# Four transposing loads in place of eight TensorE transposes, and the weights on one queue

## The chip, the cores and the metric

The kernel runs on one core of a Trainium2 chip. The metric is the device time of one execution in microseconds (us). The kernel before took 262.44 us (median of 3 runs, 262.2 to 262.47).

A core has five engines that run their own lists of instructions in order: TensorE (PE, with its weight loads listed apart as PEld), VectorE (DVE), ScalarE (ACT), GpSimd (POOL) and SyncE (SP). SP issues transfers, and ScalarE issues some beside its own work. The two have a queue each; 16 transfer engines work off both.

## What is computed

The reference mixes two branches of the same input x (2048 tokens of 512 channels, bf16) by a gate per token:

```python
x = A_x
g = _sigmoid((x * gate_w).sum(-1, keepdims=True))
a = _A_ref(x, A_wq, A_wk, A_wv, A_wo, A_beta)
b = _B_ref(x, B_w_gate, B_w_up, B_w_down)
return g * a + (1 - g) * b
```

Branch A is attention with a memory, for 32 heads of 16 channels, over four segments of 512 tokens one after the other:

```python
logits = jnp.einsum('bhqd,bhkd->bhqk', qs, ks) * scale + mask
p = _softmax(logits, axis=-1)
a_dot = jnp.einsum('bhqk,bhkd->bhqd', p, vs)
pq = phi(qs)
num = jnp.einsum('bhld,bhde->bhle', pq, M)
den = jnp.einsum('bhld,bhd->bhl', pq, z)[..., None] + 1e-06
a_mem = num / den
o = g * a_mem + (1.0 - g) * a_dot
...
pk = phi(ks)
M = M + jnp.einsum('bhld,bhle->bhde', pk, vs)
z = z + jnp.einsum('bhld->bhd', pk)
```

Branch B is a gated feed-forward layer: `h = gelu(x @ w_gate) * (x @ w_up)`, and `h @ w_down`, with 1792 hidden channels.

## The kernel before

**Tiling.** The work is split into the four segments s = 0 to 3 of 512 tokens. x is needed with channels on the partitions: `xT` holds it as four blocks kb of 128 channels by 512 tokens. For each segment there are tasks by name: `K{s}_{t}`, `Q{s}_{t}`, `V{s}_{t}` (projections, t = 0 to 3), `G{s}_{ft}` and `U{s}_{ft}` (gate and up projections, 14 each), `qk{s}_{t}...` (fills of scores into four PSUM banks called psXALL, five for each t that is even and four for each odd one), `exp...` (ScalarE, 128x2048 at a time), `msk...` (GpSimd), `pv...` (probabilities times V), `norm...`, `mz`, `numx` and `num` (memory), and `D`, `R` (down and output projections). The other four PSUM banks, psW, are shared by all other results. `...ev` tasks copy a result out of PSUM to SBUF.

**Order.** Every task is created by `_build`, and `ORDER` (L43 to L144) lists by hand, for each engine, in which order its tasks run, and so which of ScalarE and VectorE does each copy. `Sched.schedule` (L269) goes along these lists to give out the PSUM banks; it uses a table of assumed landing times, `LANDING` (L39), for the first transfers. `Emitter` (L349 on) derives the semaphore waits from what each task reads and writes. Every engine works in order, so that an instruction that waits holds all behind it.

**Tiling modes of TensorE.** Fills of scores, `numx` and the row pieces `R` use 32 rows of the array at a time; `pv` and `mz` use 32 columns at a time. `Sched.column_runs` also splits the wide matmuls of a stretch between two fills by columns when the stretch holds a `pv` or `mz` (L543 in the profile instead of L541). `Sched.change` names what counts as a change of mode.

**The head.** While x and the weights come in, TensorE runs eight matmuls on constants (`warm0` to `warm7`, L635). The first segment's x is loaded as plain rows into `xin` (four blocks of hT[1]) by two transfers, `x0_0` for tokens 0 to 255 and `x0_1` for tokens 256 to 511 (L578). Each half is transposed by TensorE with eight 128x128 matmuls into psXALL (`x0t0a_u`, `x0t0b_u`, `x0t1_u`, L644) and copied into `xT` by VectorE and ScalarE (`x0ev...`, L651 and L652). K of this segment is computed in pieces of 256 columns, so that a piece needs one half u of x only: `K0_t.0` and `.1` are blocks 0 and 1 of the first half, `.2` and `.3` of the second, `.4` and `.5` blocks 2 and 3 of the first, `.6` and `.7` of the second. `Q0_t` goes to psXALL, in 512 columns; `Q0_t.0` needs the first half of wq, `Q0_t.2` the second. The first fill of scores, `qk0_0A0`, needs all of psXALL free again.

wk comes in three transfers (`w_wk0`, `w_wk1`, `w_wk2`), wq and wv in two. SP issues x0_0, x0_1, w_wk2, w_wq1, w_wv1, then the first half of w_gate (w_wg0), the x of the next segment as four transposing loads (`x1_0` to `x1_3`, L574), the gate's weights `gwb` and `beta`, and the second half of w_gate. ScalarE issues w_wk0, w_wk1, w_wq0 and w_wv0.

`xin` is read a second time: VectorE multiplies it with gwb (`gmul0`, L806), and the row sums of that give the gate.

Of the kernel before, what the change touches and what calls it, by code (L numbers as in the profile page):

```python
# [21 lines left out]
P = 128  # L22
# [17 lines left out]
    "x0_0": 4.35, "w_wk0": 4.15, "x0_1": 5.6, "w_wk1": 5.45, "w_wk2": 6.6, "w_wq0": 7.0, "w_wq1": 8.4, "w_wv0": 9.2,  # L40
    "w_wv1": 10.2, "w_wg0": 12.2, "x1_0": 12.9, "w_gwb": 13.2, "x1_1": 13.8, "w_beta": 14.1, "x1_2": 14.4, "x1_3": 14.8,
# [1220 lines left out]
```

## Time and profile before

| | |
|---|---|
| median of the runs | 262.44 us (262.2, 262.44, 262.47) |
| profiled execution | 262.03 us |
| its span, first to last instruction | 260.8 us |
| granted TensorE clock, mean | 1.0 |
| TensorE busy, 0 to 10 us | 8.73 us |
| TensorE busy, 10 to 20 us | 9.95 us |
| first transpose of x0 | 4.52 us |
| first matmul of K0, of Q0 | 5.19 us, 8.18 us |
| first fill of scores, first exp | 13.35 us, 13.80 us |

The first transfers, with the time at which each was issued and how much later it had landed:

| transfer | queue | issued | landed after |
|---|---|---|---|
| x0_0, 256 KB | SP | 0.82 | 3.7 |
| w_wk0, 128 KB | ACT | 0.87 | 3.4 |
| w_wk1, 128 KB | ACT | 1.30 | 4.2 |
| x0_1, 256 KB | SP | 1.32 | 4.4 |
| w_wk2, 256 KB | SP | 1.82 | 5.3 |
| w_wq0, 256 KB | ACT | 1.82 | 5.5 |
| w_wq1, 256 KB | SP | 2.33 | 6.3 |
| w_wv0, 256 KB | ACT | 2.34 | 6.6 |
| w_wv1, 256 KB | SP | 2.84 | 6.7 |
| w_wg0, 896 KB | SP | 3.35 | 8.7 |
| x1_0, transposing | SP | 3.87 | 8.7 |

In the views, a row of the timeline begins with its start and length in us; then follow engine, source line, operation, what it writes and reads, how many instructions were merged in it, and in brackets the idle time before it and what ended it. L541 is any wide matmul, L543 one that is split by columns, L920 a fill of scores, L1088 a row piece.

### The profile page before, as it was taken

The numbers are of one execution on the slowest core, as the hardware profiler recorded it, in microseconds if no ns is written. First come the engines' busy times: TensorE is split into PE (matmuls) and PEld (weight loads), VectorE is DVE, ScalarE is ACT, GpSimd is POOL, SyncE is SP. The second block draws the span as 40 slices with busy tenths as digits, with TensorE's granted clock in tenths as the row PEclk, the third lists the DMA queues.
The fourth block names the chain that finished last, engine by engine and source line by source line (L and its number), as shares of the span: only waits on it lengthen the run. The fifth ranks groups of instructions, "written<-read, shape, count | busy, mean of one in ns | idle before, by whom it ended". The sixth has DMA issues, their size and how long they took to land.

```text
span 260.8 us, 10396 instructions
## 1 busy us (share of the span) xinstructions
PE 254.2 (97%) x4653; PEld 126.9 (49%) x4674; DVE 183.8 (70%) x348; ACT 212.4 (81%) x191; POOL 104.8 (40%) x260
## 2 busy tenths in 40 slices
PE   8999999999999999999999999999999999999996
PEld 3544354444553664534454563544455445454454
DVE  0688789989997616989889307899898301598563
ACT  4699899899999969988849867889988878877722
POOL 8206484878000544193800008548310128526430
DMA  7963263069049022190005303020000300320002
GB/s 217 318 173 61 45 186 103 3 213 195 3 49 238 14 53 63 23 124 3 3 3 120 64 5 92 15 85 1 3 4 14 93 5 0 85 64 3 3 3 83
DMA packets 32780, 18.43 MB, mean 71 GB/s; under 512 B 20576, under 2 KB 32736, under 8 KB 32736
## 3 DMA queue, kind: packets, MB, share of 16 engines
q1 hardware_dynamic: 31904, 16.99, 27.8%
q8 instruction: 36, 0.59, 0.9%
q10 hardware_dynamic: 832, 0.79, 0.9%
q14 instruction: 8, 0.07, 0.1%
HBM read 9.84 MB, written 2.10 MB: 46 GB/s over the span
## 4 chain that ended last, share of the span: by engine, by line
PE 89%; DVE 4%; ACT 2%; DMA 1%; issue 1%; POOL 0%; ACTq 0%
PE psW L541 33%; PE psW L543 24%; PE psW L1088 14%; PE psXALL L920 8%; PE psW L968 5%; PE psXALL L543 2%; DMA hT<-in_A_x_dram 1%; PE psXALL L541 1%; ACT pt L926 1%; DVE hT L564 1%; PE psW L976 1%; DVE tb L982 1%; ACT ptl L926 1%; PE psXALL L839 1%; DVE glog L814 0%
## 5 line engine op out<-in xcount | busy, mean ns | idle before, releaser
L926 ACT ACTIVATE pt<-psXALL 128x2048 bf16<-128x2048 f32 x64 | 120.1, 1877 | 25.7 <-PE psXALL L920 23.0
L929 POOL TENSOR_SCALAR_AFFINE_SELECT pt<-pt 128x256 bf16<-128x256 bf16 x128 | 57.5, 461 | 82.9 <-ACT pt L926 77.8
L929 POOL TENSOR_SCALAR_AFFINE_SELECT ptl<-ptl 128x512 bf16<-128x512 bf16 x32 | 23.1, 721 | 52.7 <-ACT ptl L926 51.0
L1067 DVE TENSOR_TENSOR hT<-psW,hT 128x512 bf16<-128x512 f32 x56 | 36.9, 682 | 9.0 <-PE psW L541 7.8
L1088 PE MATMUL psW<-wd,hT 32*128 32x512 bf16 x576 | 34.8, 374 | 0.0
L982 DVE STREAM_TRANSPOSE tb<-psW 128x512 f32<-128x512 f32 x32 | 22.3, 706 | 9.9 <-PE psW L976 9.8
L541 PE MATMUL psW<-xT,wu 128*128 128x512 bf16 x111 | 28.1, 380 | 1.2 <-issue 0.8
L1117 DVE TENSOR_SCALAR ost<-psW,omgt 128x512 bf16<-128x512 f32 x8 | 5.8, 747 | 32.7 <-PE psW L541 31.1
L541 PE MATMUL psW<-xT,wg 128*128 128x512 bf16 x112 | 28.0, 380 | 0.6 <-issue 0.3
L920 PE MATMUL psXALL<-qT,kpad 32*128 32x320 bf16 (+3 forms) x512 | 25.6, 272 | 0.4 <-ACT ptl L926 0.2
L543 PE MATMUL psW<-xT,wu 128*32 128x512 bf16 x424 | 25.9, 379 | 0.0
L543 PE MATMUL psW<-xT,wg 128*32 128x512 bf16 x432 | 25.4, 379 | 0.0
L1088 PEld LDWEIGHTS psW<-wd,hT 32*128 32x128 bf16 x576 | 18.9, 93 | 10.4
L1051 ACT ACTIVATE hT<-psW 128x512 bf16<-128x512 f32 x28 | 15.5, 596 | 6.5 <-PE psW L543 6.0
L920 PEld LDWEIGHTS psXALL<-qT,kpad 32*128 32x128 bf16 x512 | 8.8, 92 | 22.1 <-ACT pt L926 16.0
L968 PE MATMUL psW<-pt,vaug 128*17 128x192 bf16 (+3 forms) x512 | 19.2, 273 | 0.0
L541 PEld LDWEIGHTS psW<-xT,wu 128*128 128x128 bf16 x118 | 10.5, 98 | 13.6 <-issue 1.2
L541 PEld LDWEIGHTS psW<-xT,wg 128*128 128x128 bf16 x116 | 10.5, 98 | 13.0 <-issue 1.9
L968 PEld LDWEIGHTS psW<-pt,vaug 128*17 128x17 bf16 x512 | 11.8, 91 | 9.5 <-issue 0.8
L543 PEld LDWEIGHTS psW<-xT,wu 128*32 128x32 bf16 x424 | 10.9, 97 | 10.3 <-issue 0.4
L926 ACT ACTIVATE ptl<-psXALL 128x2048 bf16<-128x2048 f32 x8 | 15.0, 1880 | 1.0 <-PE psXALL L920 0.8
L543 PEld LDWEIGHTS psW<-xT,wg 128*32 128x32 bf16 x432 | 10.6, 97 | 10.1 <-issue 0.4
(124 smaller groups left out, 385.4 us busy)
## 6 DMA issues: line engine op xcount, KB each, us to landing
out_dram<-ost SPq DMA_DIRECT2D x15, 128.0 KB, 1.8
wg<-in_B_w_gate_dram SPq DMA_DIRECT2D x2, 896.0 KB, 7.2
wu<-in_B_w_up_dram SPq DMA_DIRECT2D x2, 896.0 KB, 6.8
wd<-in_B_w_down_dram SPq DMA_DIRECT2D x2, 896.0 KB, 5.9
phkt<-in_A_x_dram SPq DMA_DIRECT2D x3, 512.0 KB, 4.5
vlow<-vaug SPq DMA_DIRECT2D x8, 136.0 KB, 2.9
hT<-in_A_x_dram SPq DMA_DIRECT2D x2, 256.0 KB, 4.0
wo<-in_A_wo_dram SPq DMA_DIRECT2D x1, 512.0 KB, 6.2
```

The lines of the kernel that those rows point to most:

```text
L541: return e.matmul(view(), lhsT, rhs, start=first, stop=last)
L543: r = e.matmul(view()[c:c + 32, :], lhsT[:, c:c + 32], rhs, start=first, stop=last, tile_position=(0, c))
L564: alts[DVE] = [Instr(lambda e: e.tensor_copy(dst(), src()), reads=reads, writes=writes, est=dve_t(n))]
L920: instrs.append(Instr(lambda e, g=g, lhs=lhs, rhs=rhs, c0=c0, ncol=ncol: e.matmul(X[g][:, c0:c0 + ncol], lhs(32 * g), rhs(32 * g), start=T ...
L926: exp_task(s, f"exp{s}_{t}{name}", [Instr(lambda e: e.activation(dst[:], XALL[:, :].rearrange("p (g c) -> p g c", g=4), ACTF.Exp, scale=AT ...
L929: task(f"msk{s}_{t}{name}", POOL, [Instr(lambda e, view=view, pat=pat, base=base: e.affine_select(out=view, in_=view, compare_op=ALU.is_ge ...
L968: instrs.append(Instr(lambda e, t=t, q=q, kb=kb, slot=slot, c0=c0: e.matmul(gp.f32()[32 * q:32 * q + 17, 128 * kb + 64:512], Vaug[sl][:, k ...
L982: task(f"pvt{s}_{t}_{j}", DVE, [Instr(lambda e: e.transpose(Tb[:, j, :], gp.f32()[:, :]), [gp.key], [("Tb", j)], 0.71)], grp=gp)
L1051: lambda e, g=g, ft=ft, s=s: e.activation(hT[s % 2][:, ft, :], g.f32()[:, :], ACTF.Gelu_apprx_tanh),
L1067: task(f"Um{s}_{ft}", DVE, [Instr(lambda e, g=g, ft=ft: e.tensor_tensor(hT[sl][:, ft, :], g.f32()[:, :], hT[sl][:, ft, :], ALU.mult), [g.k ...
L1088: return Instr(lambda e: e.matmul(gs[tile].f32()[:, :], a[32 * r:32 * r + 32, :], b[32 * r:32 * r + 32, :], start=False, stop=False, tile_ ...
L1117: DVE: [Instr(lambda e: e.tensor_scalar(ost[:], g.f32()[:, :], omgt[:, gt:gt + 1], None, ALU.mult), rd, wr, dve_t(512, ap=True))]}, grp=g))
```

## The change

The second half of x0 goes into `xT[0][:, kb, 256:512]` by four transposing loads `x0T_0` to `x0T_3`, one for each block of 128 channels, which SP issues directly behind x0_0. The three TensorE tasks that transposed it and their copies are gone. `x0_1` remains, since gmul0 reads it, but SP issues it behind w_wg0 and x1_0. All pieces of wk, wq and wv are issued by ScalarE, so that it issues seven transfers instead of four. Every list of `ORDER` is another one, and `LANDING` holds other assumed times.

```diff
-    for u in range(2):
+    rank[0] -= 20000.0
+    dma("x0_0", SP, lambda: xin[:, 0:2, :], lambda: A_x[0, 0:256, :].rearrange("(a p) d -> p a d", p=P), [],
+        [("hT", 1, a) for a in range(2)], 250000, bias=rank[0], issue=0.5)
+    for wkey, i, dst, src in wloads:
+        wdma((wkey, i), ACT, dst, src, 250000, issue=0.5)
+    for kb in range(4):
         rank[0] -= 20000.0
-        dma(f"x0_{u}", SP, lambda u=u: xin[:, 2 * u:2 * u + 2, :],
-            lambda u=u: A_x[0, u * 256:(u + 1) * 256, :].rearrange("(a p) d -> p a d", p=P), [],
-            [("hT", 1, 2 * u + a) for a in range(2)], 250000, bias=rank[0], issue=0.5)
-        for wkey, i, dst, src in wloads[u:u + 1] if u == 0 else wloads[1:]:
-            wdma((wkey, i), SP if (wkey, i) in (("wk", 2), ("wq", 1), ("wv", 1)) else ACT, dst, src, 250000,
-                 issue=0.5)
+        dma(f"x0T_{kb}", SP, lambda kb=kb: xT[0][:, kb, 256:512],
+            lambda kb=kb: A_x[0, 256:512, kb * 128:(kb + 1) * 128], [], [("xT", 0, kb, 1)], 87500,
+            issue=0.7, transpose=True, bias=rank[0])
     wdma(("wg", 0), SP, wg[:, :, 0:half], wgr[:, :, 0:half], 790000)
-    xdma(1, 0, 2)
+    xdma(1, 0, 1)
+    rank[0] -= 20000.0
+    dma("x0_1", SP, lambda: xin[:, 2:4, :], lambda: A_x[0, 256:512, :].rearrange("(a p) d -> p a d", p=P), [],
+        [("hT", 1, 2 + a) for a in range(2)], 250000, bias=rank[0], issue=0.5)
+    xdma(1, 1, 2)
...
-    for nm, u, k0, nk, c0 in (("0a", 0, 0, 1, 0), ("0b", 0, 1, 1, 1024), ("1", 0, 2, 2, 2048),
-                              ("0a", 1, 0, 1, 3072), ("0b", 1, 1, 1, 1280), ("1", 1, 2, 2, 512)):
+    for nm, u, k0, nk, c0 in (("0a", 0, 0, 1, 0), ("0b", 0, 1, 1, 1024), ("1", 0, 2, 2, 2048)):
...
-        held = [("x0ps", c0) for c0 in ((0, 512), (1024, 1280), (2048,), (3072,))[t]] if x else []
+        held = [("x0ps", c0) for c0 in ((0,), (1024,), (2048,), ())[t]] if x else []
```

The lists of TensorE in the head, up to the first fill, and in the stretch of row pieces of the last segment, the old ones first:

```diff
-        "warm0 warm1 warm2 warm3 warm4 warm5 warm6 warm7 x0t0a_0 x0t0b_0 x0t1_0 K0_0.0 K0_2.0 K0_3.0 K0_1.0 "
-        "x0t0a_1 x0t0b_1 K0_3.1 K0_0.1 K0_2.1 x0t1_1 K0_1.1 K0_1.2 K0_3.2 K0_0.2 K0_1.3 K0_1.4 K0_1.5 K0_1.6 "
-        "K0_1.7 K0_0.3 K0_0.4 K0_0.5 K0_0.6 K0_0.7 Q0_3.0 Q0_0.0 K0_3.3 Q0_2.0 Q0_3.2 Q0_2.2 K0_2.2 K0_2.3 Q0_1.0 "
-        "Q0_0.2 Q0_1.2 V0_2.0 V0_2.2 K0_2.4 K0_2.5 K0_2.6 K0_2.7 qk0_0A0 V0_0.0 G0_2.0 V0_0.2 G0_2.2 K0_3.4 V0_1.0 "
+        "warm0 warm1 warm2 warm3 warm4 warm5 warm6 warm7 x0t0a_0 x0t0b_0 x0t1_0 K0_0.0 K0_2.0 K0_3.0 K0_1.0 K0_3.1 "
+        "K0_0.1 K0_2.1 K0_1.1 K0_1.2 K0_3.2 K0_0.2 K0_1.3 K0_0.3 K0_1.4 K0_1.5 K0_0.4 K0_0.5 K0_3.3 K0_2.2 K0_2.3 "
+        "K0_2.4 K0_2.5 K0_1.6 K0_0.6 K0_1.7 K0_0.7 Q0_3.0 Q0_0.0 Q0_2.0 Q0_3.2 Q0_2.2 Q0_1.0 Q0_0.2 Q0_1.2 V0_2.0 "
+        "V0_2.2 K0_2.6 K0_2.7 qk0_0A0 V0_0.0 G0_2.0 V0_0.2 G0_2.2 K0_3.4 V0_1.0 qk0_0B0 K0_3.5 K0_3.6 V0_1.2 "
...
-        "R2.0.2 R2.0.4 qk3_0B0 R2.0.6 R2.0.8 R2.0.10 R2.0.12 R2.0.14 qk3_0L R2.1.2 R2.1.4 R2.1.6 R2.1.8 R2.1.10 "
-        "qk3_0A1 R2.1.12 R2.1.14 R2.2.2 R2.2.4 qk3_0B1 R2.2.6 R2.2.8 R2.2.10 R2.2.12 R2.2.14 qk3_1A0 R2.3.2 R2.3.4 "
+        "U2_2.0 U2_2.2 qk3_0A0 U3_3.0 U3_3.2 D2_2.0 D2_3.0 D2_1.0 D2_0.0 R2.0.2 R2.0.4 qk3_0B0 R2.0.6 R2.0.8 "
+        "R2.0.10 R2.0.12 R2.0.14 qk3_0L R2.1.2 R2.1.4 R2.1.6 R2.1.8 R2.1.10 R2.1.12 R2.1.14 qk3_0A1 R2.2.2 R2.2.4 "
+        "R2.2.6 R2.2.8 R2.2.10 R2.2.12 R2.2.14 qk3_0B1 R2.3.2 R2.3.4 R2.3.6 R2.3.8 R2.3.10 qk3_1A0 R2.3.12 R2.3.14 "
```

The other lists differ in the same manner: tasks of the same names in another order, and some copies moved between ScalarE and VectorE. ScalarE's list has 188 tasks instead of 181, VectorE's 239 instead of 246.

More of the change, by code (lines that the diff above doesn't have):

```diff
@@ L39 @@
 LANDING = {
-    "x0_0": 4.35, "w_wk0": 4.15, "x0_1": 5.6, "w_wk1": 5.45, "w_wk2": 6.6, "w_wq0": 7.0, "w_wq1": 8.4, "w_wv0": 9.2,
-    "w_wv1": 10.2, "w_wg0": 12.2, "x1_0": 12.9, "w_gwb": 13.2, "x1_1": 13.8, "w_beta": 14.1, "x1_2": 14.4, "x1_3": 14.8,
+    "x0_0": 4.4, "w_wk0": 4.3, "w_wk1": 4.9, "x0T_0": 5.4, "x0T_1": 5.8, "w_wk2": 6.4, "x0T_2": 6.5, "x0T_3": 7.0,
+    "w_wq0": 7.3, "w_wq1": 8.4, "w_wv0": 9.2, "w_wv1": 10.0, "w_wg0": 12.4, "x1_0": 12.9, "x0_1": 13.6, "w_gwb": 13.9, "x1_1": 14.5,
+    "w_beta": 14.8, "x1_2": 15.1, "x1_3": 15.5,
 }
@@ L638, in _build @@
     XB = XALL.bitcast(BF)
-    for nm, u, k0, nk, c0 in (("0a", 0, 0, 1, 0), ("0b", 0, 1, 1, 1024), ("1", 0, 2, 2, 2048),
-                              ("0a", 1, 0, 1, 3072), ("0b", 1, 1, 1, 1280), ("1", 1, 2, 2, 512)):
+    for nm, u, k0, nk, c0 in (("0a", 0, 0, 1, 0), ("0b", 0, 1, 1, 1024), ("1", 0, 2, 2, 2048)):
         src = XB[:, c0:c0 + 256 * nk].rearrange("p (k c) -> p k c", c=256)
         key = ("x0ps", c0)
-        keys = [key, ("x0ps", c0 // 1024 * 1024)] if c0 in (512, 1280) else [key]
         task(f"x0t{nm}_{u}", PE, [Instr(lambda e, k=k, a=a, u=u, k0=k0, src=src: e.transpose(
             src[:, k, a * 128:(a + 1) * 128], xin[:, 2 * u + a, (k0 + k) * 128:(k0 + k + 1) * 128],
-            ident[:, :]), [("hT", 1, 2 * u + a), ("c", "ident")], keys, mm_t(128))
+            ident[:, :]), [("hT", 1, 2 * u + a), ("c", "ident")], [key], mm_t(128))
             for k in range(nk) for a in range(2)])
```

165 rows, old and new, of the table ORDER are left out of this document.

## The prediction

> **What bounds the kernel.** I read the page's first part and its chain, then the timeline of TensorE from 4 to 8.6 us.
>
> ```profile
> PE 254.2 (97%) x4653; PEld 126.9 (49%) x4674; DVE 183.8 (70%) x348; ACT 212.4 (81%) x191; POOL 104.8 (40%) x260
> PE 89%; DVE 4%; ACT 2%; DMA 1%; issue 1%; POOL 0%; ACTq 0%
> ```
>
> TensorE is busy for 97% of the span and makes 89% of the chain. So whatever leaves TensorE's list, or makes it wait, counts almost in full. The head, where the change sits:
>
> ```profile
> 4.52 0.62 PE L644 MATMUL psXALL<-ident,hT 128*128 128x128 bf16 x8 [0.31 <-DMA hT<-in_A_x_dram]
> 5.19 0.61 PE L541 MATMUL psW<-xT,wk 128*128 128x256 bf16 x4
> 5.75 0.40 PE L644 MATMUL psXALL<-ident,hT 128*128 128x128 bf16 x4
> 5.99 0.49 PE L541 MATMUL psW<-xT,wk 128*128 128x256 bf16 x3
> 6.31 0.39 PE L644 MATMUL psXALL<-ident,hT 128*128 128x128 bf16 x4
> 6.54 1.80 PE L541 MATMUL psW<-xT,wk 128*128 128x256 bf16 x14
> 8.18 0.59 PE L541 MATMUL psXALL<-xT,wq 128*128 128x512 bf16 x2
> ```
>
> Rows overlap, because matmuls are pipelined; the pace is read from start to start. The two rows x4 on L644 are the transposes of the second half of x0. Two waits stand between them, in the weight loads of TensorE (wait in brackets):
>
> ```profile
> 5.75 0.23 PEld L644 LDWEIGHTS psXALL<-ident,hT 128*128 128x128 bf16 x4 [0.23 <-DMA hT<-in_A_x_dram]
> ...
> 7.18 0.33 PEld L541 LDWEIGHTS psW<-xT,wk 128*128 128x128 bf16 x4 [0.21 <-DMA wk<-in_A_wk_dram]
> ```
>
> **What goes.** Eight transposes: 5.75 to 5.99 and 6.31 to 6.54, 0.24 + 0.23 = 0.47 us. Three x matmuls of 256 columns take 5.99 to 6.31, 0.107 each. The four after 5.19 would end at 5.62, and TensorE goes on at 5.75: about 0.1 us of waiting for x0_1 (issued at 1.32, landed 4.4 us later). Of 6.54 to 8.18, 14 x 0.107 = 1.50 is work and 0.14 the wait for the last piece of wk. Both waits can go, if what takes their place lands in time. Sum: 0.47 + 0.1 + 0.1 = 0.67 us, of which I take 0.65. The three copies out of PSUM that go with the transposes (about 0.3 to 0.4 us each on VectorE and ScalarE) count nothing: they lie beside matmuls.
>
> **What must land in time.** Counting pieces of K0 at 0.109 from 5.19 along the new list, TensorE asks for x0T_0 at 6.06, x0T_1 at 6.39, the last piece of wk at 6.61, x0T_2 at 7.59, x0T_3 at 7.81, the first half of wq at 8.03 and its second at 9.3. The trace has no half-size transposing load. The nearest rows are the full-size ones:
>
> ```profile
> L574 SPq DMA_TRANSPOSE xT<-in_A_x_dram x12: 1150/1340/2424, 3.9 to 112.0; - x12
> L574 SPq DMA_TRANSPOSE phkt<-kT x12: 1189/1262/2309, 23.9 to 161.3; - x12
> ...
> DMA to landing us min/median/max: 2.4/2.8/8.7
> ```
>
> One keeps SP for 1.2 us in quiet (min/median/max in ns) and lands 2.4 to 2.8 us after its start; with a backlog in the queues it kept SP for 1.83 (at 3.87) and 2.42 (at 6.38). For half the size the bounds are 0.6 us (in proportion) and 1.83 (no gain by size, and backlog). I take 0.7, near proportion, because at 1.3 us nothing but x0_0 is ahead on SP's queue. Then the four start at 1.32, 2.0, 2.7, 3.4; the last would land at 6.2 if the transfer engines were free.
>
> They are not, so count their time. Both windows are of the DMA view, 6 to 8 us and 13 to 13.6 us:
>
> ```profile
> DMA packets 721, 0.70 MB, mean 348 GB/s; under 512 B 42, under 2 KB 721, under 8 KB 721
> q1 hardware_dynamic: 380, 0.37, 57.9%
> q10 hardware_dynamic: 341, 0.32, 49.2%
> ```
>
> ```profile
> DMA packets 666, 0.16 MB, mean 271 GB/s; under 512 B 666, under 2 KB 666, under 8 KB 666
> ```
>
> In the first, 679 packets of 1 KB go in 2 us on 16 engines: 47 ns each, and the two queues (q1 is SP's, q10 ScalarE's) take turns. In the second a transposing load alone moves packets of 256 B: 14.4 ns each. One x0T is 64 KB, 256 packets, 16 per engine: 0.23 us. If the queues share time evenly, one takes about 0.5 us beside the weights; x0_0's data are through at about 3.8 (it lands at 4.5), so the four are through at 4.3 to 5.8 and land 0.8 to 1.3 us later (as x0_0 and x1_0 did, an estimate), by 5.4, 5.9, 6.4 and 7.0. Each is in time. The last piece of wk then lands at 6.4 to 7.1, against 7.14 before and a need at 6.61: this is the tightest. ScalarE's three extra issues, 0.5 each by its own rows, end near 4.4, before its first copy at 4.96. SP issues the first part of w_gate about 0.8 later than at 3.35, and the rest of the head follows 0.4 to 1.3 us later; TensorE first used w_gate at 14.1 (landed 12.1) and the next segment's x near 19 (landed 14.5). x0_1 now arrives near 13.6, and VectorE's product with it started at 14.06. So these cost nothing; if that cover is gone, VectorE starts it some 0.4 us late, and behind it wait the copies of G0_2 and V0_0 and the PSUM banks that they free.
>
> **The new orders.** TensorE loses about 0.1 us wherever the tiling changes: after four matmuls at 12.82 (0.43) the row-tiled one starts at 13.35; after its 0.21 the next starts at 13.68. By the kernel's rule there are 124 such changes in the old list and 126 in the new (row-tiled neighbours not counted): +2 x 0.11 = +0.22. Between two fills of the scores ScalarE needs one exp, and the fill at 211.09 is followed by the next at 213.53: 2.44 us is the floor, with too little TensorE work between. Adding up the work in each stretch, 11 stretches are below 2.45 in the old list (1.33 us short in all) and 11 in the new (1.22): -0.1. ScalarE gets five more copies net, at 0.5 to 0.6 each; they cost nothing while TensorE still has work before the next fill, up to 0.5 us if five of them delay an exp by 0.1. I take +0.2 of that: together +0.1. The tail (last chunks, three finishes, two stores) keeps its order.
>
> Sum: -0.65 + 0.22 + 0.1 = -0.33 us. The profiled execution took 262.03 (span 260.8), 0.41 below the median 262.44: 261.7 on its own scale, **262.1** on the median's. Differences of 0.2% (0.52 us) are about what can be told from none, so this is "no difference", just.
>
> **Rivals.**
> *The transposing loads come last (slower).* If the queues alternate packet by packet, each x0T goes at the pace of 16 pairs, 16 x (47 + 14.4) = 0.98 us. The four are through at 4.8, 5.8, 6.8, 7.8 and land at 5.6 to 9.1; TensorE, in order, waits for x0T_1 and then for x0T_3 (8.6 to 9.1 against 7.81), 0.8 to 1.3 us in all. Net -0.33 + 0.8..1.3 = +0.5 to +1.0: 262.9 to 263.4. It decides for slower from a landing of x0T_3 at 8.7. The same comes if SP needs 1.83 for each: the last is issued at 6.8, lands at 9.2 or later, +1.1 or more. For it: nothing shows the queues to share time; with equal packets the row 6 to 8 fits both. Against: SP's queue is nearly empty then.
> The Trainium skill, DMA: Bandwidth & Descriptors, section Queues, rings and completion order, states that each DMA engine goes round the queues packet by packet; by that this rival's time would come out, if a packet there is one of these rows' packets. No run here has unequal packets in both queues at once.
> *A weight takes the wait over.* Once x0T is through, w_gate's 1792-byte packets share with wq and wv, which were ahead of it before. Half of the time each would bring wq near 8.6 and 10 instead of 8.03 and 9.3: 0.4 to 0.7 us, net about 0 to +0.4: 262.4 to 262.8. It shares its chance with new waits of the new lists in general.
> *The lists help too.* The wait of 0.5 us at 211 to 213 goes (the new list has seven row pieces there, not four), without new ones: -0.65 - 0.5 + 0.22 = -0.9, 261.5.
>
> **Chances.** Forecast 0.33, late transposing loads 0.32, weights or new waits 0.15, better lists 0.20. Of the forecast's own range (261.7 to 262.6) 0.09 is faster by over 0.2%, with the 0.20 of the better lists; of the first rival 0.25 is slower by over 0.2%, of the second 0.11. Faster 0.29, same 0.35, slower 0.36. Range 261.4 to 263.7: the slow end has x0T_3 1.6 us late. Cases of both signs hold most of it.
>
> **What would show it.** Right: no L644 after 5.2, Q0 from about 8.0 with five more K0 pieces done, the first fill at 12.7 instead of 13.35, and the same shift at every later stage. Late loads: weight loads waiting for xT between 6 and 9 us, released by a transposing load. Weights: waits on wk or wq at 6.6 to 10. Lists: the shift shrinks or grows after 20 us, in stretches between fills. Wrong altogether: a stall elsewhere in the head, on w_gate or on the x of the next segment.

## The result, and the profile after

The changed kernel takes **264.6 us** (median of 6 runs, 264.38 to 265.0). The kernel before, run beside it, takes 262.15 us (6 runs, 261.75 to 262.47). The ratio is 1.0097, with a 95% interval of 1.0083 to 1.0111: slower by 2.45 us. The prediction was 262.1, with a range up to 263.7.

The profiled execution of the changed kernel took 265.0 us, the highest of the six; its span is 263.8 us at a granted clock of 1.0. Against the profiled execution of before the span is 3.0 us longer, and TensorE's last matmul ends 2.16 us later (260.94 after, 258.78 before). The other 0.8 us lies behind the last matmul; the last experiment deals with it.

First the page of the changed kernel: busy time of each engine, and the shares of the chain that ended last.

```profile
PE 253.9 (96%) x4585; PEld 126.3 (48%) x4609; DVE 181.6 (69%) x341; ACT 215.4 (82%) x196; POOL 106.0 (40%) x260
PE 82%; ACT 7%; DVE 3%; issue 2%; DMA 2%; SPq 1%; POOL 0%; ACTq 0%; DVEq 0%
```

TensorE is busy for 0.3 us less than before, since transposes went, and waits more: its share of the chain fell from 89% to 82%. The timeline of TensorE from 4 to 11 us shows where (start, length, operation, and in brackets the idle time before the row and what ended it; lines have moved by some, and L540 is the wide matmul):

```profile
5.13 1.94 PE L540 MATMUL psW<-xT,wk 128*128 128x256 bf16 x11
8.13 1.38 PE L540 MATMUL psW<-xT,wk 128*128 128x256 bf16 x11 [1.07 <-DMA xT<-in_A_x_dram]
10.16 0.63 PE L540 MATMUL psW<-xT,wk 128*128 128x256 bf16 x4 [0.65 <-DMA xT<-in_A_x_dram]
10.62 0.59 PE L540 MATMUL psXALL<-xT,wq 128*128 128x512 bf16 x2
```

No transpose follows the first eight. But the 26 pieces of K0 fall into three groups, and before the second and the third TensorE waits for xT, from a transfer: for x0T_1 and for x0T_2. Q0 starts at 10.62 instead of 8.18, the first fill of scores at 15.25 instead of 13.35.

The timeline of SP shows the four issues in one row, and below it stands the group of all its transposing loads of x (duration in ns, min/median/max, then first and last start):

```profile
1.32 5.05 SPq L573 DMA_TRANSPOSE xT<-in_A_x_dram  x4
```

```profile
L573 SPq DMA_TRANSPOSE xT<-in_A_x_dram x16: 1122/1242/3191, 1.3 to 103.4; - x16
```

Four half-size issues take 5.05 us, 1.2 to 1.3 each: no less than a full-size one. They land at 6.15, 8.09, 10.11 and 10.35, though the last was issued at 5.13. The weights on ScalarE's queue were not late: w_wk2 landed at 5.64 (7.14 before), w_wq0 at 6.92 (7.36), w_wq1 at 7.88 (8.65).

**The loss adds up.** The prediction had worked out when TensorE asks for each load: 6.06, 6.39, 7.59 and 7.81. With these landings the first makes it wait 0.09 us. The second is asked for at 6.48 and lands at 8.09: 1.61. The third is asked for at 7.59 + 1.70 = 9.29: 0.82. The fourth at 7.81 + 2.52 = 10.33: 0.02. The sum is 2.54 us, and the predicted first fill of 12.70 (13.35 - 0.65) plus 2.54 is 15.24; measured, 15.25.

The split of this sum is not what the trace has, though its end is. In this execution the first six matmuls of K0 start 0.21 us apart, half the pace of the others (0.109); before, K0 ran at 0.11 from its start. So eleven matmuls take 1.94 us in the first row, TensorE comes to the first piece that needs x0T_0 only at 6.58, when it has landed, and to the one that needs x0T_1 at 6.90. Counted from start to start, it waits 1.23 us there and 0.81 for x0T_2, together 2.0; the other 0.5 is the slow start. As x0T_1 landed after both 6.48 and 6.90, the slow start costs nothing here. With loads in time it would have cost this execution about 0.5 us of the saving.

From the first fill on the shift of 1.90 is carried to the end, where it is 2.16; in between it lies at 0.8 to 4.1, as the new lists put work in other stretches, and it comes back.

So four transposing loads were late, and the question is why. Three theories stood at first. Theory A: ScalarE's packets, running beside the loads, hold them up. The second: four transposing loads need this long by themselves, each having a fixed cost of about 1.2 us at the issue. The third: the move of the weights to one queue, or the new lists, costs the time.

### The profile page after: what moved, and what is told of

It reads as the page before. It is cut to its first block, busy times and chain, and to the rows that moved or that the text cites. A ratio compares the mean times of both kernels' runs of the same rounds, so it can differ in the third digit from the quotient of the medians.

```text
span 263.8 us, 10275 instructions
## 1 busy us (share of the span) xinstructions
PE 253.9 (96%) x4585; PEld 126.3 (48%) x4609; DVE 181.6 (69%) x341; ACT 215.4 (82%) x196; POOL 106.0 (40%) x260
## 4 chain that ended last, share of the span: by engine, by line
PE 82%; ACT 7%; DVE 3%; issue 2%; DMA 2%; SPq 1%; POOL 0%; ACTq 0%; DVEq 0%
PE psW L540 31%; PE psW L542 21%; PE psW L1091 14%; PE psXALL L923 7%; ACT pt L929 4%; PE psW L971 4%; DMA xT<-in_A_x_dram 2%; PE psXALL L542 2%; PE psXALL L540 1%; PE psW L979 1%; DVE tb L985 1%; SPq L573 1%; ACT ptl L929 1%; PE psXALL L842 1%; PE psW L889 1%
## 5 line engine op out<-in xcount | busy, mean ns | idle before, releaser
L932 POOL TENSOR_SCALAR_AFFINE_SELECT ptl<-ptl 128x512 bf16<-128x512 bf16 x32 | 24.0, 748 | 33.4 <-ACT ptl L929 31.6
L540 PE MATMUL psW<-xT,wu 128*128 128x512 bf16 x125 | 31.6, 380 | 1.1 <-issue 0.8
L542 PE MATMUL psW<-xT,wg 128*32 128x512 bf16 x528 | 31.8, 380 | 0.0
L1120 DVE TENSOR_SCALAR ost<-psW,omgt 128x512 bf16<-128x512 f32 x9 | 6.7, 748 | 28.4 <-PE psW L540 27.1
L540 PE MATMUL psW<-xT,wg 128*128 128x512 bf16 x88 | 23.1, 380 | 0.5 <-DVE tb L985 0.2
L542 PE MATMUL psW<-xT,wu 128*32 128x512 bf16 x368 | 22.2, 380 | 0.0
L540 PE MATMUL psW<-xT,wk 128*128 128x512 bf16 (+1 forms) x73 | 16.9, 344 | 2.2 <-DMA xT<-in_A_x_dram 1.7
L540 PEld LDWEIGHTS psW<-xT,wu 128*128 128x128 bf16 x132 | 11.8, 98 | 14.9 <-issue 1.5
L542 PEld LDWEIGHTS psW<-xT,wg 128*32 128x32 bf16 x528 | 12.8, 97 | 12.3 <-ACT hT L1054 1.2
L971 PEld LDWEIGHTS psW<-pt,vaug 128*17 128x17 bf16 x512 | 11.6, 91 | 10.1 <-POOL pt L932 1.2
L829 POOL COPY exsT<-exs 32x4 f32<-32x4 f32 x64 | 12.8, 201 | 4.4 <-ACT exs L820 0.8
```

Of the source, the lines that this page charges most:

```text
L540: return e.matmul(view(), lhsT, rhs, start=first, stop=last)
L542: r = e.matmul(view()[c:c + 32, :], lhsT[:, c:c + 32], rhs, start=first, stop=last, tile_position=(0, c))
L829: cross = task(f"exsT{s}", POOL, [Instr(lambda e, g=g, c=c: e.tensor_copy(exsT[sl][32 * g:32 * g + 32, c:16:4], exs[32 * c:32 * c + 32, s4 ...
L932: task(f"msk{s}_{t}{name}", POOL, [Instr(lambda e, view=view, pat=pat, base=base: e.affine_select(out=view, in_=view, compare_op=ALU.is_ge ...
L971: instrs.append(Instr(lambda e, t=t, q=q, kb=kb, slot=slot, c0=c0: e.matmul(gp.f32()[32 * q:32 * q + 17, 128 * kb + 64:512], Vaug[sl][:, k ...
L1120: DVE: [Instr(lambda e: e.tensor_scalar(ost[:], g.f32()[:, :], omgt[:, gt:gt + 1], None, ALU.mult), rd, wr, dve_t(512, ap=True))]}, grp=g))
```

## The experiments

**1. The queues alone.** The kernel before, with TensorE's transposes and the old lists, but wk, wq and wv all issued by ScalarE.

```diff
-            wdma((wkey, i), SP if (wkey, i) in (("wk", 2), ("wq", 1), ("wv", 1)) else ACT, dst, src, 250000,
+            wdma((wkey, i), ACT, dst, src, 250000,
```

> The kernel before, with one thing changed: all seven pieces of wk, wq and wv are issued by ScalarE, in the order in which the changed kernel has them (SP issues x0_0, x0_1, then w_gate). Theory (only the transposing loads are late): no loss from the queue; the last piece of wk lands near 6 us instead of 7.1, the wait for it goes, 261.9 to 262.3. Rival (the queue is the loss, since w_gate now shares with wq and wv from 5 us on): wq lands after 8 us, TensorE waits 0.5 us or more for it, 262.6 to 264.

Measured: 263.61 us against 261.96 beside it, ratio 1.0067 (1.0048 to 1.0087). So by itself the move of the weights loses about 1.65 us. SP now issues w_gate at 1.82, and its packets run beside those of the weights. The DMA view of this run from 5.6 to 7.8 us (packets, MB, share of the 16 engines; q1 is SP's queue, q10 ScalarE's):

```profile
q1 hardware_dynamic: 295, 0.53, 67.1%
q10 hardware_dynamic: 294, 0.28, 39.5%
```

295 packets of w_gate, 1792 B each, beside 294 of the weights, 1 KB each: equal counts, unequal bytes. This is the run with unequal packets in both queues that the prediction missed: they alternate packet by packet. The Trainium skill (DMA: Bandwidth & Descriptors, section Queues, rings and completion order) states that; the trace agrees. The last piece of wk lands at 8.15 instead of 7.14, wq at 9.50 and 10.41, and TensorE waits:

```profile
8.19 1.16 PE L539 MATMUL psW<-xT,wk 128*128 128x256 bf16 x9 [0.58 <-DMA wk<-in_A_wk_dram]
9.55 1.04 PE L539 MATMUL psXALL<-xT,wq 128*128 128x512 bf16 x4 [0.20 <-DMA wq<-in_A_wq_dram]
```

The first fill comes 1.55 us late, every later fill 1.55 to 1.86, the last matmul 1.69: with the old lists a loss in the head goes to the end almost unchanged. In the changed kernel this loss does not occur: the slow issues of the transposing loads keep w_gate back until 6.42.

**2. The lists alone.** The old head (transfers, transposes, K0 to Q0 up to the first fill), with the new lists behind it.

```diff
-        "Q0_0.2 Q0_1.2 V0_2.0 V0_2.2 K0_2.4 K0_2.5 K0_2.6 K0_2.7 qk0_0A0 V0_0.0 G0_2.0 V0_0.2 G0_2.2 K0_3.4 V0_1.0 "
-        "qk0_0B0 K0_3.5 V0_3.0 K0_3.6 K0_3.7 G0_4.0 V0_3.2 G0_4.2 qk0_0L V0_1.2 V1_1.0 Q1_2.0 V1_1.2 Q1_2.2 "
...
+        "K0_2.3 Q0_1.0 Q0_0.2 Q0_1.2 V0_2.0 V0_2.2 K0_2.4 K0_2.5 K0_2.6 K0_2.7 qk0_0A0 V0_0.0 G0_2.0 V0_0.2 "
+        "G0_2.2 K0_3.4 V0_1.0 qk0_0B0 K0_3.5 K0_3.6 V0_1.2 V0_3.0 V0_3.2 K0_3.7 G0_4.0 qk0_0L G0_3.0 G0_3.2 "
...
```

> The new lists alone: the head up to the first fill of scores, its transfers and its TensorE transposes are those of the kernel before, everything behind it runs in the order of the changed kernel. Theory (the loss is in the head): first fill at 13.35, end 0 to 0.5 us later than before, 262.2 to 262.6. Rival (the new lists cost most of the 2.45 us): 263.5 or more.

Measured: 262.49 us, ratio 1.002 (1.0007 to 1.0033). First fill 0.26 us later than before, last matmul 0.52: the lists cost **0.26 us** between the two. In the changed kernel it is the same, 2.16 - 1.90. The prediction had 0.32. The 0.26 us of the head are not the lists' doing: x0_1 landed at 5.67 (5.71 before) and the last piece of wk at 6.53 (7.14), but in this execution too the first four matmuls of K0 start 0.21 us apart. So the third theory is out: the lists cost too little, and what the queues alone cost (w_gate beside wq) does not occur in the changed kernel.

**3. Quiet queues.** The changed kernel, with wq, wv and w_gate held back until the last x0T has landed.

```diff
-        wdma((wkey, i), ACT, dst, src, 250000, issue=0.5)
+        wdma((wkey, i), ACT, dst, src, 250000, issue=0.5) if wkey == "wk" else None
...
+    for wkey, i, dst, src in wloads[3:]:
+        wdma((wkey, i), ACT, dst, src, 250000, issue=0.5, reads=[("xT", 0, 3, 1)])
-    wdma(("wg", 0), SP, wg[:, :, 0:half], wgr[:, :, 0:half], 790000)
+    wdma(("wg", 0), SP, wg[:, :, 0:half], wgr[:, :, 0:half], 790000, reads=[("xT", 0, 3, 1)])
```

> The changed kernel, but wq, wv and w_gate are issued only when the last of the four transposing loads has landed, so that after wk nothing shares the transfer engines with them. It is for the landing times, not for the total: wq comes late here. Theory A (the traffic of ScalarE's queue holds the transposing loads up): they land 1.25 us apart, as SP issues them, the last at 7.6 to 8.2 instead of 10.35; TensorE then waits for wq until about 10.7, total near 264.5. Theory B (they are slow by themselves, one after the other): they land 2 us apart as before, the last near 10, wq near 12.5, total 266 to 267.

Measured: 269.65 us, ratio 1.029 (1.0269 to 1.031). The loads land at 6.01, 6.21, 6.41 and 7.46, with the same slow issues (started from 1.32 to 5.12, 1.2 each). Each is in time for the needs of the prediction. K0, which began 0.14 us earlier here, waits 0.13 us for x0T_0 and for nothing else:

```profile
5.05 3.15 PE L540 MATMUL psW<-xT,wk 128*128 128x256 bf16 x26
12.69 0.61 PE L540 MATMUL psXALL<-xT,wq 128*128 128x512 bf16 x1 [4.49 <-DMA wq<-in_A_wq_dram]
```

So the slow issue, which I had mis-sized, costs nothing; the traffic beside the loads does. Theory A holds for the landings, and the theory of the issues falls. The total was missed by far: wq landed at 12.64 and 15.55, since its first packets left only at 9.96 and w_gate takes turns with it, and behind a wait of 4.5 us TensorE ran at half speed (see the end).

**4. Two loads instead of four.** Each with 128 tokens and all 512 channels.

```diff
-    for kb in range(4):
+    for i in range(2):
         rank[0] -= 20000.0
-        dma(f"x0T_{kb}", SP, lambda kb=kb: xT[0][:, kb, 256:512],
-            lambda kb=kb: A_x[0, 256:512, kb * 128:(kb + 1) * 128], [], [("xT", 0, kb, 1)], 87500,
+        dma(f"x0T_{i}", SP, lambda i=i: xT[0][:, :, 256 + 128 * i:384 + 128 * i],
+            lambda i=i: A_x[0, 256 + 128 * i:384 + 128 * i, :], [], [("xT", 0, kb, 1 + i) for kb in range(4)], 175000,
```

> The changed kernel with two transposing loads of 128 tokens x 512 channels in place of four of 256 tokens x 128 channels: the same bytes in half as many issues. TensorE does the pieces of K0 of the first half first. Theory (each transposing load has a fixed cost, of SP and of landing, whatever its size): they land near 6.1 and 8.1, Q0 starts near 9.0, first fill near 13.9 instead of 15.25, 263.0 to 263.5. Rival (the bytes set it): the last lands near 10.3 and the time stays at 264.3 to 264.7.

Measured: 264.07 us, ratio 1.0081 (1.0061 to 1.0101). The loads land at 6.81 and 9.49, TensorE waits 1.88 us for the second, Q0 starts at 10.49. The last landing lies between the two forecasts (8.1 and 10.3), nearer to the rival's. Half as many issues gain little, which speaks against the theory of the issues once more.

**5. Larger packets of the weights.** Theory A, taken as turns packet by packet and nothing else, still had to say why the loads take so long: their data lie side by side with ScalarE's, but SP's queue also shows pauses of 0.55 to 0.65 us in which it moves nothing between two loads (4.35 to 4.90, 7.16 to 7.76, 8.36 to 9.00). In this run wq and wv come in packets of 2 KB.

```diff
+    two = lambda src, h: src[256 * h:256 * h + 256, :].rearrange("(p j) n -> p j n", j=2)
-    wloads = [(wkey, i, w[:, k0:k1, :], r4(src)[:, k0:k1, :])
+    wloads = [(wkey, i, w[:, k0:k1, :], r4(src)[:, k0:k1, :] if wkey == "wk" else two(src, i))
```

> The changed kernel, but wq and wv come in packets of 2 KB instead of 1 KB (two neighbouring rows of the weight on one partition; so the rows of wq and wv lie on other partitions than those of x, and this part of the computation is changed; the bytes, the matmuls and their number are the same). Theory A (the queues alternate packet by packet): a packet of 256 B behind one of 2 KB waits twice as long, so from wq on the transposing loads get later: with 256 packets beside 256 of 2 KB on 16 engines, 16 x (94 + 14) ns = 1.7 us instead of 1.0 for a load that lies wholly beside wq or wv. x0T_1, whose second half lies beside wq, lands at 8.5 to 9.0 (8.09 in the changed kernel), x0T_2 at 10.3 or later (10.11). Theory B (the queues share the time or the bytes): the loads land where they did, within 0.2 us, or earlier because fewer packets stand in line. Total 264.5 to 266 by A, 264.0 to 265 by B; the landings decide, not the total.

Measured: 264.82 us, ratio 1.0113 (1.0095 to 1.013). The loads land at 6.09, 7.79, 9.63 and 9.86: the last three 0.3 to 0.5 earlier, not later. That is what theory B allowed, yet the queues did take turns by packets: from 5.36 to 7.03, while x0T_1's data ran, SP's queue moved 282 packets and ScalarE's 270. Turns alone don't explain the landings. But the weights too were 0.3 to 0.5 earlier (w_wq1 7.54, w_wv1 9.24), and the loads had moved along with them: a first sign of what experiments 8 to 11 show.

**6. Part of the weights behind the loads.** ScalarE issues only wk and w_wq0; SP issues w_wq1, w_wv0 and w_wv1 behind the four loads.

```diff
-        wdma((wkey, i), ACT, dst, src, 250000, issue=0.5)
+        wdma((wkey, i), SP if (wkey, i) in (('wq', 1), ('wv', 0), ('wv', 1)) else ACT, dst, src, 250000, issue=0.5)
```

> The changed kernel, its new lists included, but ScalarE issues only wk and the first half of wq, and SP issues the second half of wq and both halves of wv, behind the four transposing loads and ahead of w_gate. Theory A (the loss comes from the packets of ScalarE's queue that run beside the transposing loads): ScalarE's traffic is through near 6.0, the loads land at about 6.1, 7.2, 7.6 and 8.0 (6.15, 8.09, 10.11, 10.35 in the changed kernel), TensorE waits 0.5 to 0.9 us in all, Q0 starts near 8.9 (10.62), first fill of the scores near 13.5 (15.25, before 13.35), total 262.3 to 262.9. Theory C (four transposing loads one behind another take this long whatever runs beside them): landings stay at 8.1 and 10.1 or later, total 264 or more. Rival for the total: wq's second half and wv, now issued after 6.4, land near 9.5 to 10.5, behind their need at 9.9 (wq) and 11 (wv); then the fill comes at 14 or later and the total is 263 or more.

Measured: 265.18 us, ratio 1.0121 (1.0106 to 1.0136). In the head all came as expected: loads at 6.08, 7.27, 7.48 and 7.68, Q0 at 8.96, first fill at 13.59. But then TensorE waits, and the gain is gone (its timeline, and that of its weight loads):

```profile
16.01 0.60 PE L540 MATMUL psW<-xT,wg 128*128 128x512 bf16 x2 [1.48 <-DMA wg<-in_B_w_gate_dram]
```

```profile
16.00 0.11 PEld L540 LDWEIGHTS psW<-xT,wg 128*128 128x128 bf16 x2 [1.98 <-DMA wg<-in_B_w_gate_dram]
```

w_gate, issued at 8.06, lands at 15.96, against a need at 14.1: the cover that the prediction had named (first use at 14.1) is gone. Its packets also went slowly, 211 GB/s from 10.4 to 12.2 us, where the changed kernel moved it at 380 (340 packets from 10 to 11.6); why stays open.

**7. wv behind the copies.** The old lists behind the head; K0 takes the first token half of all blocks first, so that the loads are needed from 6.9 us; ScalarE issues wv only behind its two copies of the first half (at 5.28), SP issues w_wq1 behind the loads.

```diff
-        wdma((wkey, i), ACT, dst, src, 250000, issue=0.5)
+        wdma((wkey, i), SP if (wkey, i) in (('wq', 1),) else ACT, dst, src, 250000, issue=0.5)
...
-               for ks in ((0, 1), (2, 3)) for u, c in enumerate(cols) for kb in ks]
+               for ks in (((0, 1, 2, 3),) if nu > 1 else ((0, 1), (2, 3))) for u, c in enumerate(cols) for kb in ks]
```

> Four transposing loads as in the changed kernel, with the old lists behind the head. ScalarE issues wk and the first half of wq, and wv only after its two copies of the first token half; SP issues the second half of wq behind the transposing loads, then x0_1, the gate's bias row and w_gate. K0 takes the first token half of all four blocks first, then the second half. So no large packets of weights run beside the later transposing loads, and they are needed later. Theory A: the loads land at about 6.1, 7.2, 7.6 and 8.0, the first of them needed near 6.9, K0 ends near 8.3 to 8.9, first fill at 12.7 to 13.1 (before: 13.35), total 261.4 to 261.9 against about 262.0 for the kernel before. Rival: what the transposing loads free on TensorE is taken by later arrivals (x0_1 for the gate's product on VectorE, wv, w_gate: each lands 1 to 3 us later than before), first fill at 13.4 or later, total 262.2 to 263.

Measured: 263.85 us, ratio 1.0087 (1.0062 to 1.0113). The loads land at 6.21, 7.57, 7.83 and **9.56**: the last one beside wv, which was to be out of its way and was not. TensorE waits 1.34 us for it. Its weight loads then wait 0.59 us more for w_wq1, which now stands behind the loads and lands at 11.34. First fill is at 14.95.

**8 and 9. w_gate on ScalarE's queue.** To mend experiment 6, ScalarE issues w_gate behind its two copies (at 5.4 to 5.5); experiment 9 adds the order of K0 and the old lists of experiment 7.

```diff
-    wdma(("wg", 0), SP, wg[:, :, 0:half], wgr[:, :, 0:half], 790000)
+    wdma(("wg", 0), ACT, wg[:, :, 0:half], wgr[:, :, 0:half], 790000)
```

> As the run with the second half of wq and wv on SP's queue, with its new lists, but the first part of w_gate is issued by ScalarE, behind its two copies of the first token half (near 5.3), instead of by SP behind wv (8.06). Theory A: what that run lost behind the first fill of the scores (+2.3 us) is the wait for w_gate, which landed at 15.96; the transposing loads still land by 7.7, the first fill comes at 13.5 to 13.9, w_gate lands near 12.5, no wait for it at 14, and the total is 262.2 to 262.9 (265.2 in that run). Rival: w_gate now takes turns with the second half of wq and with wv, so these land 0.7 to 1.7 us later than 9.47, 10.21 and 11.15; Q0 or V0 waits, first fill 14.3 or later, total 263.0 to 264.

> The same queues as the run with w_gate on ScalarE, with K0 taking the first token half of all four blocks before the second half (so that the transposing loads are needed from 6.9 instead of 6.1), the old lists behind the head, and x0_1 with the gate's bias row ahead of the next segment's x on SP's queue. Theory A: K0 ends near 8.5 without waiting for a transposing load, first fill 12.9 to 13.3 (before: 13.35), total 261.4 to 262.0, against about 261.9 for the kernel before. Rival: wq's second half or wv, sharing packet by packet with w_gate, come 0.3 us or more behind their need (about 10.3 and 12.0); first fill 13.5 or later, total 262.1 to 263.

Measured: 265.81 us, ratio 1.0167 (1.0126 to 1.0208), and 266.77 us, ratio 1.0187 (1.017 to 1.0203). Neither theory had expected it: x0T_3, issued at 5.13, lands at 11.49 and 11.48, right behind w_gate (11.28 in both), which was issued after it. The DMA view of experiment 8 from 7.6 to 9.6 us has one queue only, ScalarE's:

```profile
DMA packets 376, 0.67 MB, mean 337 GB/s; under 512 B 0, under 2 KB 376, under 8 KB 376
...
q10 hardware_dynamic: 376, 0.67, 100.1%
```

The packets of 256 B, all 1024 of the four loads, were through at 7.48. What x0T_3 still lacked were its semaphore writes (packets of 4 B), and they leave from 9.96 on, with those of w_gate. The wait of TensorE in experiment 8:

```profile
11.53 0.11 PEld L540 LDWEIGHTS psW<-xT,wk 128*128 128x128 bf16 x2 [2.18 <-DMA xT<-in_A_x_dram]
```

This gave **theory D**: beside another queue's transfer, a transposing load writes its semaphores, and the next one starts its data, only where a transfer of the other queue ends. The packet records of the changed kernel fit it. The ends on ScalarE's queue (16 semaphore packets each) leave at 4.90 to 5.03 (w_wk2), 6.17 to 6.60 (w_wq0), 6.99 to 7.15 (w_wq1), 7.75 to 8.12 (w_wv0) and 9.00 to 9.04 (w_wv1). Those of x0T_0, x0T_1 and x0T_2 (32 each) leave at 4.90 to 5.04, 7.00 to 7.15 and 9.00 to 9.05; the data of x0T_2 had been through at 8.34. The data of x0T_2 began at 7.76, in the moment in which the first semaphore packet of w_wv0 left (7.75). Between 8.4 and 8.9 us, with the data of x0T_2 through and x0T_3 issued, SP's queue has no packet; the DMA view of the changed kernel shows ScalarE's alone:

```profile
DMA packets 146, 0.15 MB, mean 299 GB/s; under 512 B 0, under 2 KB 146, under 8 KB 146
...
q10 hardware_dynamic: 146, 0.15, 94.2%
```

Experiment 7 has it too: the data of x0T_3 begin at 7.69, where wv's first half ends (7.69 to 7.76), and its semaphores leave at 8.62 to 8.68, with those of the second half (8.61 to 8.67).

**10. Smaller transfers.** wq and wv in four transfers of 128 KB each.

```diff
-              for wkey, w, src, cuts in (("wk", wk, A_wk, (0, 1, 2, 4)), ("wq", wq, A_wq, (0, 2, 4)),
-                                         ("wv", wv, A_wv, (0, 2, 4)))
+              for wkey, w, src, cuts in (("wk", wk, A_wk, (0, 1, 2, 4)), ("wq", wq, A_wq, (0, 1, 2, 3, 4)),
+                                         ("wv", wv, A_wv, (0, 1, 2, 3, 4)))
```

> The changed kernel with wq and wv loaded in four transfers of 128 KB each instead of two of 256 KB; the same bytes, packets and queue, and the last three of wv are issued behind ScalarE's two copies of the first token half. Theory D, formed after the runs so far: a transposing load writes its semaphores, and the next one starts its data, only when a transfer of ScalarE's queue beside it ends (in the changed kernel the semaphores of x0T_1 leave at 7.00 to 7.15 and those of wq's second half at 6.99 to 7.15; x0T_2 at 9.00 to 9.05 and wv's last at 9.00 to 9.04, 0.66 us after the last data of x0T_2). With transfers half as long the pauses halve: data of x0T_2 start near 7.3 (7.76) and its semaphores leave by 8.6 (9.0), it lands by 9.7 (10.11), x0T_3 by 10.1 (10.35); total 263.9 to 264.5. Theory A alone (turns packet by packet, nothing else): only the count of packets matters, which is unchanged; landings as in the changed kernel within 0.2 us, total 264.3 to 265.

Measured: 264.42 us, ratio 1.0091 (1.0074 to 1.0108). Data of x0T_2 from 6.82 (7.76 in the changed kernel), its semaphores at 7.71 to 7.79, together with those of a piece of wq (7.72 to 7.78), landed at 8.77 (10.11). Theory A alone had no change here. The total lies in both forecasts and doesn't tell them apart; the landings do. x0T_3, however, gains little: it begins at 7.85, shares with wv until 8.86 and lands at 10.19 (10.35).

**11. Larger transfers.** wq and wv in one transfer of 512 KB each: `("wq", wq, A_wq, (0, 4))`, and the same for wv.

> The changed kernel with wq and wv loaded in one transfer of 512 KB each instead of two of 256 KB; the same bytes, packets and queue. Theory D (a transposing load ends, and the next begins, only where a transfer of ScalarE's queue ends): those ends are now near 7.1 (wq) and 9.0 (wv) alone. x0T_1 ends at 7.1 as before, but the data of x0T_2 begin at 9.0 instead of 7.76, the semaphores of x0T_2 at 9.25 or later and its landing at 10.3 to 10.5, x0T_3 0.2 to 0.4 later; total 264.5 to 265.3. Theory A alone: data of x0T_2 begin near 7.8 as in the changed kernel, total within 0.3 us of it (264.6), or less because ScalarE issues two transfers fewer.

Measured: 266.62 us (264.43 to 267.4, ratio 1.0165, 1.012 to 1.0211); the profiled execution was the one of 264.43. In the other three the mean granted clock is 0.993 to 0.994 instead of 1.0, as in all four of experiment 9; so the median belongs to executions with another clock than the traced one, and neither theory had forecast it. From 7.4 to 8.4 us SP's queue moves next to nothing while wv runs:

```profile
q10 hardware_dynamic: 323, 0.33, 109.4%
q1 hardware_dynamic: 4, 0.00, 0.3%
```

The data of x0T_2 begin at 8.46, when wv's first semaphore packet leaves (8.46), not at 7.8 as A alone had it. D had said 9.0; wv was done earlier than I thought, and so the landings are 9.79 and 10.03, not 10.3 and later: even 0.3 earlier than in the changed kernel. The place at which the data begin is D's; the forecast of later landings failed.

**The sum in every run.** Six of the runs that keep the order of K0, and are held up by these loads, are in the table. For each the needs of the prediction and the measured landings give a delay, worked out as above, and 12.70 plus the delay is the first fill:

| run | x0T land at | delay | 12.70 + delay | first fill |
|---|---|---|---|---|
| changed kernel | 6.15, 8.09, 10.11, 10.35 | 2.54 | 15.24 | 15.25 |
| 5, larger packets | 6.09, 7.79, 9.63, 9.86 | 2.05 | 14.75 | 14.76 |
| 6, weights behind | 6.08, 7.27, 7.48, 7.68 | 0.88 | 13.58 | 13.59 |
| 8, w_gate on ACT | 6.43, 7.99, 8.23, 11.49 | 3.68 | 16.38 | 16.40 |
| 10, small transfers | 6.34, 7.57, 8.77, 10.19 | 2.38 | 15.08 | 15.09 |
| 11, large transfers | 5.95, 8.29, 9.79, 10.03 | 2.22 | 14.92 | 14.94 |

The landings of the four loads account for the whole head, to 0.02 us. Each sum comes down to the last load that makes TensorE wait: x0T_3's landing plus 4.89 (12.70 - 7.81), or in experiment 6 x0T_1's plus 6.31. So what the table tests is the work from there to the first fill. K0 up to there without a wait is seen in experiment 3, with its last start at 7.92 after a first at 5.05.

**12. The tail.** In all profiles with the new lists it takes 2.3 to 2.9 us from the last matmul to the end, in those with the old lists (before, 1, 7, 9) 2.02 to 2.04. In the changed lists VectorE finishes the first and the third of the last three whole tiles, ScalarE the second; before it was the other way round. This run puts that back.

```diff
-        "exp3_2B1 exp3_3A0 exp3_3B0 exp3_3A1 exp3_3B1 fin3_1 fin3_30 "
+        "exp3_3A0 exp3_3B0 exp3_3A1 exp3_3B1 fin3_0 fin3_2 fin3_30 "
...
-        "norm3_2 pvt3_3_0 pvt3_3_1 norm3_3 fin3_0 fin3_2 fin3_31 "
+        "pvt3_1_0 pvt3_1_1 Um3_8 Um3_13 Um3_11 norm3_1 pvt3_2_1 pvt3_2_0 norm3_2 pvt3_3_0 pvt3_3_1 norm3_3 fin3_1 fin3_31 "
```

> The changed kernel with one thing put back: of the last three whole output tiles, ScalarE again finishes the first and the third and VectorE the second (in the changed lists it is the other way round). Theory E (the new lists also lengthen the tail): in all profiles with the new lists SP's issue of the second of the last three stores, which runs beside VectorE's finish, takes 0.7 to 1.2 us instead of 0.33, and the time from TensorE's last matmul to the end is 2.3 to 2.9 us instead of 2.02. With the old assignment the issue takes 0.33 again, the tail is 2.0 to 2.1, TensorE still ends 2.1 to 2.2 us later than before, and the total is 263.9 to 264.3. Rival: the tail is longer for the shift itself or varies by execution, not by who finishes: it stays at 2.3 to 2.9 and the total at 264.4 to 264.8.

Measured: 265.13 us, ratio 1.0115 (1.0095 to 1.0134), no gain. Theory E falls. The last three stores of whole tiles on SP, in this run:

```profile
259.56 2.15 SPq L576 DMA_DIRECT2D out_dram<-ost  x3
```

and in the kernel before:

```profile
257.33 1.32 SPq L578 DMA_DIRECT2D out_dram<-ost  x3
```

The middle issue takes 1.19 us (1.22 in the changed kernel, 0.33 before), whoever finishes the tile. Experiment 2, with the old head, has it too (0.72, and a tail of 2.34), so it comes with the lists behind the head. What makes it slow there stays open.

## Why the prediction was wrong

**What failed** is the step on the landings: "If the queues share time evenly, one takes about 0.5 us beside the weights; ... so the four are through at 4.3 to 5.8 and land 0.8 to 1.3 us later ..., by 5.4, 5.9, 6.4 and 7.0." They landed at 6.15, 8.09, 10.11 and 10.35. Two things were wrong in it. The queues don't share time, they alternate by packets (experiment 1). And a transposing load beside another queue's transfers isn't a stream of packets alone: its end and the next one's start wait for ends of those transfers (experiments 8, 10 and 11). Each x0T was issued early enough; in quiet it is in time (experiment 3).

**Rival 1** had the right mechanism and the right sign, at half the price: turns by packets, 0.8 to 1.3 us of waiting, last landing 8.6 to 9.1. Measured, 2.54 us and 10.35. What it lacked are the pauses at the transfers' ends: the data of the four loads took 3.0 us in all, against its 4 x 0.98 = 3.9, but between them lie 2.4 us (4.35 to 5.19, 6.84 to 7.76, 8.36 to 9.02). The sentence of the Trainium skill that I set beside it was true here; I gave it 0.32 because no row of before had unequal packets in both queues. Without such a row, the slow end of the range should have been worked out without any sharing: the loads behind all of ScalarE's queue, whose last transfer had landed at 9.0 before with half of the weights on it, and the last weight of all at 9.6. With x0T_3 at 9.6 or later that is 1.8 us of waiting or more, against which the range allowed 1.6.

**The issue of 0.7 us** was 1.2 to 1.3. It did not matter by itself, as experiment 3 shows; by holding w_gate back until 6.42 it even kept rival 2 from happening, which was luck.

**Rival 2** (w_gate takes turns with wq and wv) is real: experiment 1 is it, at 1.55 us. In the changed kernel w_gate's first packets leave behind the last of wv.

**The saving** of 0.65 us fits the runs: with 12.70 as the first fill without waits the table holds to 0.02 us in six runs, and experiment 3 has K0 nearly without a wait. It was never reached: in the six the loads were late, in experiment 3 wq.

**The lists**: 0.32 predicted, 0.26 measured. The shift is carried to the end, as predicted; the stretches in between move by up to 2 us and return.

**The tail**, "keeps its order", was wrong: the last three whole tiles had changed engines, which I overlooked, though that isn't what costs. It adds 0.8 us in the profiled execution, the longest of the six; of the difference of the medians 2.45 - 2.16 = 0.3 us is left for it. In experiment 2 it is 0.31 us longer than before.

Sum: -0.65 + 2.54 + 0.26 + 0.3 = +2.45 us. The last term is what is left, and not measured by itself.

## What to carry to other kernels

A transfer that replaces work on the bounding engine has to be priced at its landing, beside the traffic that will be there, and not at its own bytes: here 0.65 us of TensorE was exchanged for 2.5 us of waiting on loads of 64 KB each. Where a transposing load has to be in time, keep transfers off the other queue while it runs (experiments 3 and 6); to cut them smaller gained only 0.16 us at the first fill (experiment 10). And ask which transfer, held back for it, is late next, as w_gate was in experiment 6 and w_wq1 in experiment 7. None of the runs here beat the kernel before; an arrangement in which both the loads and w_gate are in time was not found.

## What the runs showed of the hardware

- **A transposing load ended with the other queue's transfer.** Its semaphore writes left together with those of a transfer beside it, to 0.1 us: 0.66 us after its last data beside 256 KB of wv, 2.5 us beside w_gate's 896 KB (data through at 7.48, semaphores from 9.96). With nothing beside they follow at once (experiment 3: data of x0T_3 through at 6.99, semaphores 7.02 to 7.17). Why it is so, no run shows.
- **A half-size transposing load cost SP as much as a full one**: 1.19 to 1.24 us for 256 x 128 elements in the changed kernel, where the median of all 16, twelve of them 512 x 128, is 1.24.
- **Which queue issues a transfer decides what it shares with.** The same transfers, three of them moved from SP to ScalarE, cost 1.55 us at the first fill (experiment 1): w_gate no longer stood behind them, and took turns with them.
- **Behind the two longest waits TensorE's clock was halved.** The windows of experiment 9 (window, its length, then busy time and count of PE, PEld, DVE, ACT and POOL, granted PE clock, DMA share, GB/s) around its wait for x0T_3, from 8.4 to 11.5 (3.17 us without a matmul, 3.44 without a weight load):

```profile
11.50:12.50 1.00, 0.97 (x6) 0.60 (x7) 0.02 (x1) 0.65 (x2) 0.00 (x0) 1.00 1.09 352
12.50:14.00 1.50, 1.50 (x6) 0.51 (x5) 1.45 (x5) 1.44 (x3) 0.00 (x0) 0.52 1.72 291
14.00:16.00 2.00, 2.00 (x6) 0.71 (x5) 1.44 (x4) 1.17 (x2) 0.00 (x0) 0.51 1.03 192
16.00:18.00 2.00, 2.00 (x12) 1.00 (x11) 1.19 (x3) 1.09 (x2) 0.00 (x0) 1.00 0.74 138
```

  The clock falls to 0.52 one microsecond after work has begun again and stays there for some 3.5 us; Q0's matmuls start 0.43 us apart instead of 0.215. In experiment 3, behind 4.5 us without a matmul, it is 0.50 from 12.6 to 18. Behind the wait of 1.9 us (2.2 without a weight load) in experiment 8 it stays at 1.0. The Trainium skill (TensorE: Matmul & The Clock Gate, part 1) puts the limit at an idle window of about 3.4 us; the three waits fit that roughly, with the change between 1.9 and 3.2 us without a matmul. So such a wait in the head costs more than itself: from the start of Q0 to the first fill experiment 9 takes 6.54 us, the changed kernel 4.63, and experiment 9's first fill is 4.9 us late.
